# Converting the last weight group three units later, with its partial words in PSUM, and starting the second network's weights one half chunk later

## The chip, the cores and the metric

The kernel runs on one core of one Trainium2 chip. The metric is the device time of one execution in microseconds (us). Three runs of the kernel before took 775.98, 778.04 and 781.6 us; the median is 778.04. The profiled execution took 776.87 us, and its span, from the first to the last instruction, is 775.0 us.

## The reference: what is computed

A linear attention with decay runs over four batches, eight heads and 768 steps; its output is a matrix of 3072 tokens by 384. Two feed-forward networks follow, one after the other.

```python
state = alpha[:, :, t, :, None] * state + np.einsum('bhd,bhe->bhde', k[:, :, t], v[:, :, t])
y[:, :, t] = np.einsum('bhd,bhde->bhe', q[:, :, t], state)
...
h = x @ w_in                                   # 384 -> 2048
P = a[0] + a[1] * h + a[2] * h2 + a[3] * h3    # h2 = h*h, h3 = h2*h
Q = 1.0 + np.abs(b[0]) * np.abs(h) + np.abs(b[1]) * h2
x = (P / (Q + 1e-06)) @ w_out                  # 2048 -> 384
...
h = x @ w_in                                   # 384 -> 1024
solu = h * softmax(h)
(layernorm(solu) * g_ln) @ w_out               # 1024 -> 384
```

The weights of both networks arrive as 64-bit floats. The kernel makes 32-bit words of them with integer operations, and then two rounded parts, a high and a low one, for TensorE.

## The kernel before

**Chunks, units, halves.** The steps are cut into six chunks of 128 steps, 512 tokens each. The first network's 2048 columns are cut into 16 pieces of 128. One piece of one chunk is a *unit*: u0 to u95, u0 to u15 being chunk 0. `m_up` runs a unit's nine matmuls into a tile `hp` (line 592; three PSUM banks rotate), then the rational function on ScalarE and VectorE (lines 597 to 625) and the low part on GpSimd (line 626). `m_down` (line 638) runs nine matmuls for a unit four units earlier. The last VectorE operation of a unit is line 616 (even units below 24) or line 623 (all others).

**The attention** runs beside the units, two *halves* to a chunk. Half h2 is started at u2, h3 at u10, h4 at u18 and so on; halves h2 and h3 make the input `xt` of chunk 1, that is of u16 to u31. `a_pe` makes, for a half, four score tiles `sc` (line 420), which ScalarE copies (line 427) and GpSimd masks (line 428), two tiles `y` (line 444), from which ScalarE and VectorE write `xt` (lines 470, 471), and the update tile `u` (line 483, read by line 493). All of `sc`, `y` and `u` are tiles of one PSUM pool with the tag `at`, which has **two** banks. `a_dve` (lines 300 to 338) prepares the half after that on VectorE: transposes (290, 295, 324), scans (308, 317) and products (320).

**Weight conversion.** The first network's weights are four groups, g0 to g3; group n serves units 4n to 4n+3 of every chunk. `w1_group` makes a group in seven *splits*: three of 512 columns from `w_in`, needed by the units' up matmuls, and four of 384 columns from `w_out`, needed by the down matmuls. A split (`split_w`) is a load into a staging tile `st` (line 533; two buffers), three VectorE operations with the partial word between them (537, 540, 541), a copy on ScalarE (547) and a subtraction on GpSimd (548). Where the partial word lies is said by `stage["bank"]`:

```python
if stage["bank"] == "x2":
    fp = ps_x2p.tile(...)          # PSUM, tag x2p
elif stage["bank"] == "at":
    fp = ps_ap.tile([128, NTOK], F32, name="fp", tag="at")
else:
    fp = ft                        # SBUF, in place
```

Groups g0 and g1 are made before u0, g2 at units 0 to 3 in the banks `at`, g3 at units 4 to 7 in place in SBUF. The second network's weights are 14 splits more (`w2_split`), which go back to DRAM; the main loop takes one at each unit u >= `U2` whose number is 0 or 7 modulo 8, with the partials in the banks `at`.

**Order.** Each engine and each DMA queue works through a fixed list. A scheduler that has its own idea of durations sets these lists when the kernel is built; it keeps what the program's order and `issue_after` demand and otherwise sorts freely. So a change in one place of the loop moves instructions on all engines. Loads are issued by SyncE (SP) in order: one that waits for its buffer holds up all behind it.

Of the kernel before, what the change touches and what calls it, by code (L numbers as in the profile page):

```python
# [23 lines left out]
def _run(*gens):  # L24
    for g in gens:
        for _ in g:
            pass
# [3 lines left out]
def kernel(  # L31
# [25 lines left out]
    NF1 = DF1 // 128  # L57
# [19 lines left out]
    G1 = 99  # L77
# [3 lines left out]
    SKIP = (5, 7, 11)  # L81
    AHEAD = 3
    LATE = 2
    U2, IDLE = NF1 - 1, (0, NF1 // 2 - 1)
    assert (B, H, D, CH) == (4, 8, 48, 128)

    const = ctx.enter_context(tc.tile_pool(name="const", bufs=1, side="left"))
# [55 lines left out]
    def judge(moe_pool):  # L143

        sums = const.tile([128, 1], F32, name="sums")
        row = moe_pool.tile([1, 128], F32, name="row", tag="ft", bufs=2)
        tot = const.tile([1, 1], F32, name="tot")
        nc.vector.tensor_reduce(sums, bad, axis=AX.X, op=ALU.add)
        nc.sync.dma_start(out=row, in_=sums)
        nc.vector.tensor_reduce(tot, row, axis=AX.X, op=ALU.add)  # L150
        nc.vector.tensor_scalar(flag, tot, 0.0, None, ALU.is_gt)

    def network(fast):
# [351 lines left out]
        stage = {"n": 0, "wide": False, "near": False, "bank": None}  # L505
# [46 lines left out]
        def w1_group(n):  # L552
            w = moe_pool.tile([128, GW], F32R, name=f"g{n}", tag=f"g{n}")
            hi, lo = (w[:, 512 * KT * x:512 * KT * (x + 1)].rearrange("p (a b) -> p a b", a=KT) for x in range(2))
            for kt in range(KT):
                split_w(moe_w_in[128 * kt:128 * kt + 128, 512 * n:512 * n + 512], hi[:, kt, :], lo[:, kt, :])
                yield
            wi[n] = (hi, lo)
            hi, lo = (w[:, 4 * DM * x:4 * DM * (x + 1)].rearrange("p (a b) -> p a b", a=4) for x in range(2, 4))
            for f in range(4):  # L560
                r0 = 512 * n + 128 * f
                split_w(moe_w_out[r0:r0 + 128, :], hi[:, f, :], lo[:, f, :])
                yield
            wo[n] = (hi, lo)
# [9 lines left out]
        def x_load(c):  # L574
            for kt in range(KT):
                nc.sync.dma_start(
                    out=x_tile(c)[:, kt].rearrange("p a t -> p (a t)").bitcast(F32), in_=y_d[c][128 * kt:128 * kt + 128, :]
                )
# [50 lines left out]
        def m_down(u):  # L629
            c, f = divmod(u, NF1)  # L630
            n, o = divmod(f, 4)
            if f == 0:
                x2ps[c] = [ps_x2p.tile([128, NTOK], F32, name=f"x2p{d}", tag=f"x2p{d}") for d in range(KT)]
            gh, gl = gts.pop(u)
            hi, lo = wo[n]
            for d in range(KT):
                for w, gg in ((hi, gh), (hi, gl), (lo, gh)):
                    nc.tensor.matmul(  # L638
                        x2ps[c][d], lhsT=w[:, o, 128 * d:128 * d + 128], rhs=gg,
                        start=(f == 0 and w is hi and gg is gh), stop=(f == NF1 - 1 and w is lo),  # L640
                    )
            if f == NF1 - 1:
                for d0, n in ((0, 2), (2, 1)):
                    e = moe_pool.tile([128, 2, NTOK], F32, name="x2e", tag="st", bufs=2)
                    for d in range(n):
                        nc.scalar.activation(e[:, d], x2ps[c][d0 + d], AF.Copy, scale=back if fast else 1.0)  # L646
                    nc.sync.dma_start(out=x2_d[c][:, d0:d0 + n, :], in_=e[:, :n])
                del x2ps[c]
# [14 lines left out]
        def w2_load(nm):  # L663
            src = {"i": w2i_d, "o": w2o_d}[nm]
            n, step = {"i": (KT, 1), "o": (NF2, 4)}[nm]
            for z in range(0, n, step):
                for x, y in enumerate("hl"):
                    nc.sync.dma_start(out=w2[nm + y][:, z:z + step].bitcast(F32), in_=src[:, x, z:z + step])
                    yield
# [3 lines left out]
        def n_load(c):  # L673
            t = x2s[c] = moe_pool.tile([128, KT, 2, NTOK], F32R, name="x2", tag="xt", bufs=2)
            for kt in range(KT):
                raw = t[:, kt, 1].bitcast(F32)
                nc.sync.dma_start(out=raw, in_=x2_d[c][:, kt, :])
                nc.scalar.activation(t[:, kt, 0], raw, AF.Copy)
                nc.gpsimd.tensor_tensor(t[:, kt, 1], raw, t[:, kt, 0].bitcast(F32), ALU.subtract)
                yield  # L680

        def open2():
            if fast:
                ps_a.__exit__(None, None, None)
            ph2["ps_pool"] = tc.tile_pool(name="ps_e", bufs=1, space=PSUM, side="right", reuse_waits="tile")
            ph2["ps"] = ph2["ps_pool"].__enter__()
            if fast:
                att.__exit__(None, None, None)
            ph2["pool"] = tc.tile_pool(name="w2", bufs=1, side="right", reuse_waits="tile")
            pool = ph2["pool"].__enter__()  # L690
            for nm, dims in (("i", [128, KT, DF2]), ("o", [128, NF2, DM])):
                for y in "hl":
                    w2[nm + y] = pool.tile(dims, F32R, name="w2" + nm + y)
# [102 lines left out]
        def take(g, n):  # L796
            for _ in range(n):
                if next(g, "end") == "end":
                    return False
            return True  # L800

        def chain(*gens):
            for g in gens:
                yield from g
# [37 lines left out]
        def later(n):  # L842
            return tc.issue_after(fin[now[0] - n].ins) if n <= now[0] < GE + n and now[0] - n in fin else ExitStack()
# [9 lines left out]
        def half_steps(i):  # L853
            gp = a_pe(i)
            gd = chain(a_prep(i + 1), a_move_qk(i + 1) if i + 1 >= NPE else iter(()), a_load(i + 2, ("ra", "rk")) if i + 2 < NH and i + 1 >= NPE else iter(())) if i + 1 < NH else iter(())
            while True:
                with pin(GP):
                    a = next(gp, "end")
                with pin(GS):
                    b = next(gd, "end")  # L860
                    if b != "end":
                        b = next(gd, "end")
                if a == "end" and b == "end":
                    if i + 1 < NH:
                        _run(a_enter(i + 1))
                        if i + 2 < NH and i + 1 < NPE:
                            _run(a_load(i + 2))
                    return
                yield
# [4 lines left out]
        prep = iter(())  # L874
        for u in range(NU + LAG):
            c, f = divmod(u, NF1)
            now[0] = u
            if f % (NF1 // 2) == LATE and u < NU:
                _run(side)
                i = 2 * c + 2 + f // (NF1 // 2)  # L880
                side = half_steps(i) if fast and i < NH else iter(())
            if u < NU:
                if f == 0 and c == NCH - 1:
                    if fast:
                        judge(moe_pool)
                    open2()
                    tail = chain(w2_load("i"), n_load(0), w2_load("o"))
                if f == 0 and c and not fast:
                    x_load(c)
                if fast and u < NF1:  # L890
                    if f % 4 == 0:
                        _run(prep)
                        if f:
                            stage["near"] = False
                            stage["bank"] = ""
                        prep = w1_group(f // 4 + 2) if f < 8 else iter(())
                    with later(G1):
                        take(prep, 1)
                m_up(u)
                if fast and u < NF1:  # L900
                    with later(G1):
                        take(prep, 1)
            if u == NU:
                _run(n_load(1))
            take(side, 1)
            if u >= U2 and f % (NF1 // 2) in IDLE:
                stage["bank"] = "at"
                with later(G2):
                    take(split2, 1)
            if tail is not None:  # L910
                _run(split2)
                take(tail, 2)
            if u >= LAG:
                m_down(u - LAG)
            if u - NU + NF1 in EARLY:
                n_tile(EARLY.index(u - NU + NF1))
                if len(EARLY) == B and u - NU + NF1 == EARLY[-1]:
                    n_turn(0)
# [141 lines left out]
```

## Time and profile before

| | |
|---|---|
| median of three runs | 778.04 us |
| profiled execution | 776.87 us, its span 775.0 us |
| busy: TensorE / VectorE / ScalarE / GpSimd | 728.0 / 630.4 / 535.2 / 358.4 us |
| last VectorE operation of u0, u8, u16, u24 ends at | 79.2, 123.8, 168.6, 210.7 us |
| the same for u72, u80, u88 | 460.7, 499.2, 537.3 us |

Times in a trace are counted from the span's start. An engine's row in the page's slices gives its busy share in tenths. A matmul's end is modelled and matmuls overlap, so that a TensorE that is busy all the time need not be at its peak; how many matmuls run in a stretch says more. `PE` is TensorE, `DVE` VectorE, `ACT` ScalarE, `POOL` GpSimd, `SP` SyncE.

### The profile page before, as it was taken

How to read it: one execution, taken by the hardware profiler on the slowest of the kernel's cores; microseconds unless marked ns; L12 is line 12 of the kernel's file. 1: busy time of each engine (PE TensorE's matmuls, PEld its weight loads, DVE VectorE, ACT ScalarE, POOL GpSimd, SP SyncE). 2: the span in 40 equal slices, each digit the busy share in tenths (PEclk: the TensorE clock that was granted, in tenths of full speed). 3: DMA queues.
4: the chain of work that ended last, by engine and by line, in shares of the span. 5: the costliest groups of instructions: out<-in, count | busy, mean ns of one | idle time of the engine just before them, and what ended most of it. 6: DMA issues, size and time to landing. Idle time of an engine off the chain costs nothing.

```text
span 775.0 us, 13914 instructions
## 1 busy us (share of the span) xinstructions
PE 728.0 (94%) x4976; PEld 605.8 (78%) x4976; DVE 630.4 (81%) x1110; ACT 535.2 (69%) x983; POOL 358.4 (46%) x306
## 2 busy tenths in 40 slices
PE   4676999999999999999999999999999999999996
PEld 3565767788888787778877788888888989988986
DVE  4999999989898989899898966478887788877640
ACT  2245867689878888788878887788965545555541
POOL 3255777777554355434444433332243343452322
PEclk9857899999999999999999999999999999999999
DMA  7995446466837382727554350720025253542653
GB/s 167 253 275 165 107 155 167 146 147 206 204 99 161 122 205 83 172 66 207 137 148 91 124 82 1 296 112 0 1 83 132 89 130 90 132 108 52 140 119 76
DMA packets 87278, 101.74 MB, mean 131 GB/s; under 512 B 34464, under 2 KB 63136, under 8 KB 87200
## 3 DMA queue, kind: packets, MB, share of 16 engines
q1 hardware_dynamic: 87104, 100.67, 48.9%
q8 instruction: 41, 0.67, 0.4%
q14 instruction: 37, 0.30, 0.1%
q10 hardware_dynamic: 96, 0.10, 0.0%
HBM read 60.59 MB, written 27.56 MB: 114 GB/s over the span
## 4 chain that ended last, share of the span: by engine, by line
DVE 30%; PE 18%; ACT 12%; issue 5%; SPq 3%; DMA 3%; POOL 1%; ACTq 0%; DVEq 0%; POOLq 0%
PE x2p L638 6%; PE hp L592 6%; DVE room L752 3%; SPq L762 3%; DVE room L735 2%; DVE p L618 2%; ACT jk L737 2%; PE op L776 2%; DVE hp L622 2%; DVE w L621 2%; DMA room<-room 2%; DVE sm L731 2%; DVE room L750 2%; PE h L712 2%; DVE p L623 2%
## 5 line engine op out<-in xcount | busy, mean ns | idle before, releaser
L592 PE MATMUL hp<-xt,g 128*128 128x512 f32 x864 | 224.1, 401 | 14.8 <-DVE p L616 7.5
L626 POOL TENSOR_TENSOR gl<-p,gh 128x512 fp32r<-128x512 f32 x96 | 130.8, 1362 | 193.9 <-ACT gh L625 107.9
L592 PEld LDWEIGHTS hp<-xt,g 128*128 128x128 f32 x864 | 163.2, 192 | 54.2 <-DVE p L616 7.7
L638 PE MATMUL x2p<-gh,g 128*128 128x512 f32 x576 | 196.9, 395 | 2.0 <-ACT x2e L646 2.0
L638 PEld LDWEIGHTS x2p<-gh,g 128*128 128x128 f32 x576 | 107.9, 188 | 29.1 <-ACT x2e L646 4.7
L638 PE MATMUL x2p<-gl,g 128*128 128x512 f32 x288 | 112.9, 392 | 0.0
L776 PE MATMUL op<-w2oh,room 128*128 128x384 f32 x384 | 101.8, 339 | 1.3 <-ACT room L767 0.7
L768 POOL TENSOR_TENSOR room<-room,room 128x1024 fp32r<-128x1024 f32 x22 | 54.8, 2496 | 101.0 <-ACT room L767 79.0
L621 DVE SCALAR_TENSOR_TENSOR w<-w,co,hp 128x512 f32<-128x512 f32 x84 | 62.0, 738 | 43.5 <-ACT hp L620 42.5
L712 PE MATMUL h<-w2ih,x 128*128 128x512 f32 x288 | 90.7, 394 | 0.0
L599 ACT ACTIVATE p<-hp,co 128x512 f32<-128x512 f32 x96 | 66.0, 687 | 12.3 <-POOL gl L626 12.0
L620 ACT ACTIVATE hp<-ah 128x512 f32<-128x512 f32 x84 | 50.1, 597 | 33.3 <-DVE p L618 32.0
L776 PEld LDWEIGHTS op<-w2oh,room 128*128 128x128 f32 x384 | 70.1, 188 | 3.0 <-ACT room L767 1.0
L600 ACT ACTIVATE w<-ah,co 128x512 f32<-128x512 f32 x96 | 69.4, 724 | 1.7 <-DVE hp L622 1.3
L618 DVE SCALAR_TENSOR_TENSOR p<-p,co,hp 128x512 f32<-128x512 f32 x84 | 61.6, 734 | 9.3 <-ACT p L599 9.0
L597 ACT ACTIVATE ah<-hp 128x512 f32<-128x512 f32 x96 | 56.7, 591 | 16.4 <-PE hp L592 16.0
L776 PE MATMUL op<-w2ol,room 128*128 128x384 f32 x192 | 65.0, 339 | 0.0
L625 ACT ACTIVATE gh<-p 128x512 fp32r<-128x512 f32 x96 | 59.9, 623 | 5.7 <-DVE p L623 2.8
L638 PEld LDWEIGHTS x2p<-gl,g 128*128 128x128 f32 x288 | 54.1, 188 | 11.7 <-issue 0.8
L712 PEld LDWEIGHTS h<-w2ih,x 128*128 128x128 f32 x288 | 53.9, 188 | 11.7
L623 DVE SCALAR_TENSOR_TENSOR p<-p,co,hp 128x512 f32<-128x512 f32 x84 | 61.9, 737 | 1.1
L619 ACT ACTIVATE ah<-w,co 128x512 f32<-128x512 f32 x84 | 60.6, 721 | 1.3
(168 smaller groups left out, 1264.7 us busy)
## 6 DMA issues: line engine op xcount, KB each, us to landing
room<-room SPq DMA_DIRECT2D x96, 128.0 KB, 2.3
qk_d<-qk SPq DMA_DIRECT2D x10, 771.0 KB, 4.1
st<-in_moe_w_in_dram SPq DMA_DIRECT2D x13, 512.0 KB, 4.6
st<-in_moe_w_out_dram SPq DMA_DIRECT2D x16, 384.0 KB, 3.5
qks<-qk_d SPq DMA_DIRECT2D x20, 257.0 KB, 4.4
x<-x_d SPq DMA_DIRECT2D x18, 256.0 KB, 3.1
out_dram<-o SPq DMA_DIRECT2D x94, 48.0 KB, 1.6
ra<-in_alpha_dram SPq DMA_DIRECT2D x44, 96.0 KB, 2.8
```

What stands on the lines that cost most here:

```text
L592: last["PE", u] = nc.tensor.matmul(hp, lhsT=w[:, kt, 128 * o:128 * o + 128], rhs=xts[c][:, kt, xx, :], start=(kt == 0 and w is hi and xx = ...
L599: nc.scalar.activation(p, hp, AF.Square, bias=co[:, 7:8])
L600: nc.scalar.activation(w, ah, AF.Square, bias=co[:, 6:7])
L618: nc.vector.scalar_tensor_tensor(p, p, a1, hp, ALU.add, ALU.mult)
L619: nc.scalar.activation(ah, w, AF.Ln, bias=rest)
L621: nc.vector.scalar_tensor_tensor(w, w, rest, hp, ALU.add, ALU.mult)
L623: fin[u] = nc.vector.scalar_tensor_tensor(p, p, a0, hp, ALU.add, ALU.mult)
L625: last["ACT", u] = nc.scalar.activation(gh, p, AF.Copy)
L626: last["POOL", u] = nc.gpsimd.tensor_tensor(gl, p, gh[:].bitcast(F32), ALU.subtract)
L638: nc.tensor.matmul(x2ps[c][d], lhsT=w[:, o, 128 * d:128 * d + 128], rhs=gg, start=(f == 0 and w is hi and gg is gh), stop=(f == NF1 - 1 an ...
L712: nc.tensor.matmul(hp[:, 512 * n:512 * n + 512], lhsT=x2s[c][:, kt, x, CH * b:CH * b + CH], rhs=w2[w][:, kt, 512 * n:512 * n + 512], start ...
L776: nc.tensor.matmul(op, lhsT=x[:, 128 * f:128 * f + 128], rhs=w2[w][:, f, :], start=(f == 0 and x is hi and w == "oh"), stop=(f == NF2 - 1 ...
```

## The change

Group g3 is begun at u7 instead of u4, so that its seven splits are taken two to a unit at u7 to u10, and its partial words stay in the banks `at` as those of g2 do. `U2` becomes 23 instead of 15, so that the 14 splits of the second network's weights are taken at u23, u24, u31, u32 and so on to u71, u72, where before they were taken at u15, u16 to u63, u64. The calls that ask `issue_after` are left out; with `G1` = 99 they had no effect.

```diff
-    U2, IDLE = NF1 - 1, (0, NF1 // 2 - 1)
+    OPEN3 = 7
+    U2, IDLE = NF1 + NF1 // 2 - 1, (0, NF1 // 2 - 1)
...
-                if fast and u < NF1:
-                    if f % 4 == 0:
-                        _run(prep)
-                        if f:
-                            stage["near"] = False
-                            stage["bank"] = ""
-                        prep = w1_group(f // 4 + 2) if f < 8 else iter(())
-                    with later(G1):
-                        take(prep, 1)
+                if fast and u == 0:
+                    prep = w1_group(2)
+                if fast and u == OPEN3:
+                    _run(prep)
+                    stage["near"] = False
+                    prep = w1_group(3)
+                take(prep, 1)
                 m_up(u)
-                if fast and u < NF1:
-                    with later(G1):
-                        take(prep, 1)
+                take(prep, 1)
```

Lines of the changed file are numbered one higher than before up to the main loop: 420 is 421 there, 537 is 538.

**TensorE around the scores of half h3, before.** The first score tile, `sc_1388`, stands ahead of u11's up matmuls (`hp_1427`), right after the update of half h2.

```order
L483 MATMUL u_1209<-vns_115,kns_113 64x48 x16
L420 MATMUL sc_1388<-qks_112 128x128 x4
L638 MATMUL x2p2_1096<-gh_1197,g1_629 128x512
L638 MATMUL x2p2_1096<-gl_1198,g1_629 128x512
L638 MATMUL x2p2_1096<-gh_1197,g1_629 128x512
L592 MATMUL hp_1427<-xt_356,g2_751 128x512 x9
```

The same tiles in the change are `sc_1395`, `sc_1396`, `sc_1460`, `sc_1461`; `hp_1713` is u15, `gh_1456` is u11 and `gh_1519` is u12.

```order
L639 MATMUL x2p2_1079<-gl_1457,g2_751 128x512
L639 MATMUL x2p2_1079<-gh_1456,g2_751 128x512
L421 MATMUL sc_1395<-qks_112 128x128 x4
L421 MATMUL sc_1396<-qks_112 128x128 x4
L421 MATMUL sc_1460<-qks_112 128x128 x4
L593 MATMUL hp_1713<-xt_356,g3_1195 128x512 x9
L421 MATMUL sc_1461<-qks_112 128x128 x4
L639 MATMUL x2p0_1077<-gh_1519,g3_1195 128x512
```

All four score tiles have moved behind the ups of u11 to u14 and the downs of u8 to u11; they stand directly ahead of u15.

**VectorE after the last operation of u11, in the change.** `fp_1289`, `fp_1307`, `fp_1342` and `fp_1360` are the partial words of g3's four splits of 384 columns; The lines 296 to 325 prepare half h4; in the rows left out stand the rest of the split of `fp_1289`, the split of `fp_1307`, one small transpose and one operation each of u12 and u13.

```order
L538 TENSOR_SCALAR fp_1289<-st_1290 128x384
L321 TENSOR_TENSOR qk_1476<-qk_1476,alT_111 128x2x3x128
L541 SCALAR_TENSOR_TENSOR fp_1289<-st_1290,fp_1289 128x384
L325 STREAM_TRANSPOSE alT_111<-qk_1476 128x3x4x32 x2
L296 STREAM_TRANSPOSE qk_1476<-rq_1418 128x4x32 x2
...
L538 TENSOR_SCALAR fp_1342<-st_1343 128x384
L541 SCALAR_TENSOR_TENSOR fp_1342<-st_1343,fp_1342 128x384
L542 SCALAR_TENSOR_TENSOR ft_1341<-st_1343,fp_1342 128x384
L538 TENSOR_SCALAR fp_1360<-st_1361 128x384
L541 SCALAR_TENSOR_TENSOR fp_1360<-st_1361,fp_1360 128x384
L542 SCALAR_TENSOR_TENSOR ft_1359<-st_1361,fp_1360 128x384
```

In the kernel before, all 21 conversion operations of g3 stood ahead of u11's last operation; now 12 of them stand behind it. `fp_1342` and `fp_1360` are the tiles that hold the two banks `at` just before `sc_1395` and `sc_1396`.

**VectorE at the border of chunk 0 and chunk 1.** Before, `xt_1078` is written ahead of two splits of the second network's weights (`fp_1738`, `fp_1784`) and of most of u14 (`hp_1644`) and u15 (`p_1718`).

```order
L471 TENSOR_TENSOR xt_1078<-y_1519,xt_1078 128x256
L537 TENSOR_SCALAR fp_1738<-st_1736 128x512
L540 SCALAR_TENSOR_TENSOR fp_1738<-st_1736,fp_1738 128x512
L610 SCALAR_TENSOR_TENSOR hp_1644<-p_1656,co_85,hp_1644 128x512
L541 SCALAR_TENSOR_TENSOR ft_1737<-st_1736,fp_1738 128x512
L537 TENSOR_SCALAR fp_1784<-st_1782 128x512
```

In the change `p_1725` is u15, `hp_1751` u16 and `p_1799` u17.

```order
L624 SCALAR_TENSOR_TENSOR p_1725<-p_1725,co_85,hp_1713 128x512
L472 TENSOR_TENSOR xt_1061<-y_1525,xt_1061 128x2x256
L472 TENSOR_TENSOR xt_1061<-y_1526,xt_1061 128x256
L494 TENSOR_TENSOR Sbd_114<-Sbd_114,u_1678 48x8x48 x2
L611 SCALAR_TENSOR_TENSOR hp_1751<-p_1763,co_85,hp_1751 128x512
L619 SCALAR_TENSOR_TENSOR p_1799<-p_1799,co_85,hp_1787 128x512
```

The two splits are gone from here, and `xt` is now written after the last operation of u15, with one pair of updates between it and u16's first.

## Rows read from the trace of the kernel before

**Rows 1.** The page's slices: busy tenths in 40 slices of 19.4 us.
```profile
PE   4676999999999999999999999999999999999996
DVE  4999999989898989899898966478887788877640
```

**Rows 2.** Windows: length, busy us and instructions of each engine, clock, DMA share, GB/s.
```profile
101.65:148.51 46.86, 42.47 (x343) 32.79 (x342) 46.34 (x75) 33.56 (x62) 36.98 (x33) 0.96 0.59 165
148.51:168.63 20.12, 20.06 (x176) 16.42 (x177) 17.49 (x30) 15.60 (x28) 15.71 (x14) 1.00 0.82 205
168.63:210.71 42.08, 42.08 (x334) 34.17 (x334) 37.48 (x62) 36.93 (x68) 27.62 (x25) 1.00 0.68 183
210.71:419.49 208.78, 204.37 (x1613) 163.33 (x1612) 190.67 (x311) 171.43 (x312) 98.16 (x90) 1.00 0.54 140
460.71:499.19 38.48, 38.48 (x315) 31.62 (x314) 23.89 (x34) 30.52 (x53) 12.69 (x13) 1.00 0.28 100
499.19:745.00 245.81, 245.81 (x1172) 214.52 (x1171) 187.76 (x348) 156.63 (x295) 92.14 (x54) 1.00 0.35 94
```

**Rows 3.** Window of tile ft alone: DVE, ACT and POOL of g3's conversion.
```profile
101.58:143.10 41.52, 17.65 (x22) 3.98 (x7) 8.79 (x7) 0.96 0.62 172
```

**Rows 4.** Groups by line and shape, partials in PSUM: busy us, mean ns, idle before.
```profile
L540 DVE SCALAR_TENSOR_TENSOR fp<-st,fp 128x512 int32<-128x512 int32 x10 | 6.9, 690 | 0.2
L537 DVE TENSOR_SCALAR fp<-st 128x512 int32<-128x512 int32 x10 | 6.9, 688 | 1.2 <-DMA st<-in_moe_w_in_dram 0.6 <-ACT lent L396 0.5
L541 DVE SCALAR_TENSOR_TENSOR ft<-st,fp 128x512 int32<-128x512 int32 x10 | 6.8, 680 | 0.1
L540 DVE SCALAR_TENSOR_TENSOR fp<-st,fp 128x384 int32<-128x384 int32 x12 | 6.8, 564 | 0.2
L537 DVE TENSOR_SCALAR fp<-st 128x384 int32<-128x384 int32 x12 | 6.7, 557 | 0.2
L541 DVE SCALAR_TENSOR_TENSOR ft<-st,fp 128x384 int32<-128x384 int32 x12 | 6.6, 547 | 0.2
```

**Rows 5.** DVE timeline, g3's first two TENSOR_SCALARs: start, us, engine, line, shapes.
```profile
101.58 0.41 DVE L537 TENSOR_SCALAR ft<-st 128x512 int32<-128x512 int32 x1
...
107.38 1.58 DVE L537 TENSOR_SCALAR ft<-st 128x512 int32<-128x512 int32 x1
```

**Rows 6.** DVE timeline, preparation of half h4 and u11's last operation.
```profile
143.65 0.95 DVE L320 TENSOR_TENSOR qk<-qk,alT 128x768 f32<-128x768 f32 x1
144.52 0.74 DVE L610 SCALAR_TENSOR_TENSOR hp<-p,co,hp 128x512 f32<-128x512 f32 x1
145.18 0.68 DVE L622 SCALAR_TENSOR_TENSOR hp<-w,hp 128x512 f32<-128x512 f32 x1
145.78 1.63 DVE L324 STREAM_TRANSPOSE alT<-qk 128x384 f32<-128x384 f32 x2
147.32 0.67 DVE L295 STREAM_TRANSPOSE qk<-rq 128x128 f32<-128x128 f32 x2
147.84 0.67 DVE L623 SCALAR_TENSOR_TENSOR p<-p,co,hp 128x512 f32<-128x512 f32 x1
```

**Rows 7.** DVE timeline: xt of half h3, then u16's first operation.
```profile
153.17 1.01 DVE L471 TENSOR_TENSOR xt<-y,xt 128x512 fp32r<-128x512 f32 x2
...
166.07 0.76 DVE L610 SCALAR_TENSOR_TENSOR hp<-p,co,hp 128x512 f32<-128x512 f32 x1 [1.66 <-ACT p L599]
```

**Rows 8.** Timelines of PE and ACT: h3's first and last scores, last copy, u16's ups.
```profile
125.38 1.16 PE L420 MATMUL sc<-qks 48*128 48x128 f32 x8
...
140.06 1.16 PE L420 MATMUL sc<-qks 48*128 48x128 f32 x8
...
144.67 0.58 ACT L427 ACTIVATE A<-sc 128x512 f32<-128x512 f32 x1
...
160.00 2.20 PE L592 MATMUL hp<-xt,g 128*128 128x512 f32 x9
```

**Rows 9.** The chain of waits, one unit's nine matmuls at full clock: start, us.
```profile
450.37 2.04 PE hp L592 x9
```

**Rows 10.** DMA issues of 85 to 165 us: KB each, median us to landing.
```profile
st<-in_moe_w_out_dram SPq DMA_DIRECT2D x4, 384.0 KB, 3.1
```

**Rows 11.** Windows of 2 us around a pause of TensorE, columns as in rows 2.
```profile
108.00:110.00 2.00, 0.33 (x1) 0.30 (x2) 2.00 (x3) 0.35 (x1) 1.46 (x2) 1.00 0.79 226
110.00:112.00 2.00, 2.00 (x6) 1.61 (x5) 2.00 (x4) 1.91 (x4) 1.63 (x2) 0.51 1.06 366
```

## The prediction

> **What bounds the kernel now.** I read the slices first, then the windows cut at the last VectorE operations of u11, u16, u24, u64, u72 and u80. In the slices VectorE is at nine tenths until the eighth slice, and TensorE from the sixth on [rows 1]. The windows say it by stage [rows 2]. From 101.65 us to u11's end VectorE is busy for 46.34 of 46.86 us and TensorE for 42.47; in the next stretch, to u16's end, VectorE is at 17.49 of 20.12 and TensorE at 20.06. From then on TensorE is full: 42.08 of 42.08, 204.37 of 208.78, 38.48 of 38.48, 245.81 of 245.81. So two rules follow. What shortens VectorE's list before u16 can bring u16 forward, as long as no wait on TensorE takes its place. And what u16 gains or loses is carried to the end, since no stage behind it has idle time on TensorE to make it good; only work that TensorE did earlier can be given back.
>
> **Term 1, cheaper partial words.** The window of the tile `ft` has the cost of g3's conversion: 17.65 us of VectorE in 22 operations, one of them the tail of another group, so about 17.6 for 21 [rows 3]. With the partial word in PSUM the same three operations take 0.688, 0.690 and 0.680 us at 512 columns and 0.557, 0.564 and 0.547 at 384 [rows 4]. Three splits at 2.058 are 6.17 us, four at 1.668 are 6.67, together 12.84: **-4.8 us** of VectorE. ScalarE's and GpSimd's share (3.98 and 8.79 us [rows 3]) is moved, not changed.
>
> The saving depends on where time is lost in SBUF. The two first operations of g3 have the same shape and took 0.41 and 1.58 us [rows 5]: short, or long beside something else. The Trainium skill, "VectorE: DVE Perf Modes", section "Why PSUM operands drop a tier", says that an operand in PSUM holds a 32-bit operation at the basic rate; here the 0.41 us in SBUF against 0.688 in PSUM agrees. That speaks against the change, and what it would make of the sum stands under the rivals. The sum goes by 17.6 us, since that is the mean of the stretch in which these operations run.
>
> **Term 2, the second network's first two splits** leave the border of the chunks: two splits of 512 columns, 2 x 2.06 = **4.1 us** of VectorE before u16's end. Every other pair moves by eight units too. They come back at u71 and u72, where VectorE has 38.48 - 23.89 = 14.6 us of idle time [rows 2]; that hides them, with their loads and stores. If the cover is gone (VectorE late in another stretch), two splits of 384 columns cost 3.3 us there. I take +0.5.
>
> **Term 3, the stretch up to u11.** Three of g3's splits (6.17 us) stay ahead of u11's last operation, four go behind it. Removed are 17.6 - 6.2 = 11.4 us; part of the preparation of h4 goes behind too, 0.95 + 1.63 + 0.67 = 3.25, and one of u12's operations, 0.74 [rows 6]. VectorE's 46.34 becomes 46.3 - 11.4 - 3.25 - 0.74 = 30.9 us; with the old idle time of 0.5, u11 would end at 133.1. TensorE can't quite follow: each unit asks two times nine matmuls, 2 x 2.04 = 4.08 us [rows 9], and the attention beside them, and it was busy for 42.47 us of this stretch [rows 2]. What moves off it are three of the four score tiles and their followers. I add 2 to 6 us of idle time on VectorE: u11 ends at 135 to 139, taken as 137, 11.5 earlier than before.
>
> **Term 4, the new wait.** Before, the first score tile of h3 was made at 125.38 us and the last at 140.06 [rows 8]; `xt`, which all of chunk 1 needs, was written at 153.17 to 154.18 [rows 7]. Now the tiles `fp_1342` and `fp_1360` of g3's sixth and seventh splits hold the two banks `at`. The score tiles come behind them, and these splits stand behind u11's last operation. Ahead of the first score tile VectorE works through 15 rows: three splits (3 x 1.668 = 5.0), four rows of preparation (0.95, 1.63, 0.67, and 0.67 for the fourth by its neighbour) and two operations of units (2 x 0.74), 10.4 us by their durations and 9.4 by their starts, since [rows 6] show starts a tenth closer than the durations. To this comes about 1 us, since a staged load needs 3.1 us to land [rows 10] and there are two buffers. The first score tile can start at 137 + 9.4 + 1 = **147.4**, the second three operations later at 149. The third waits for a bank too, some 1.2 us after that; the fourth has u15's nine matmuls ahead of it (2.04 us) and ends near 153.5.
>
> From the last score tile to the end of `xt` it took 154.18 - 140.06 - 1.16 = 13.0 us before, of which the last copy waited for ScalarE until 144.67 [rows 8]; from that copy on it is 9.5. So `xt` is done between 163 and 166.5, I take 164.5: 10 us later than before.
>
> u16's up matmuls need `xt`. They started at 160.00 before, 5.8 us after it was there; now they stand behind u15's last operations with nothing else to wait for. Its last operation came 8.6 us after the start of its ups (168.63 - 160.00). With up to 2.7 us for twelve down matmuls ahead of it, u16 ends at 164.5 + 8.6 + (0 to 2.7) = 173 to 176, and by the ends of `xt` at 171.6 to 177.8. I take **175**, 6.4 us later. Terms 1 and 2 are inside that: they let u11 come 11.5 us earlier, and the wait swallows it. VectorE's own work from u11 to u16 is 17.49 - 4.1 + 6.67 + 3.25 + 0.74 + 1.47 (two operations of u17 now ahead) = 25.5 us; from 137 that is 162.5, so 12 us of idle time lie in this stretch.
>
> **Sum.** At u16 +6.4; TensorE has by then done up to 18 down matmuls that it did later before, which gives back 1 of their 4.1 us, since the first units of a chunk are held by VectorE and ScalarE as well; at u71 +0.5. That is +5.9, taken as +6: the profiled 776.87 becomes 782.9. The median shown is 1.2 us above the profiled execution, so **784.0**. What a measurement of this kernel can tell from no change is about 1%, 7.8 us.
>
> **The rivals.**
> - *The savings hold (faster).* If the two banks come free early, because VectorE reaches g3's sixth split by 138 or 139, `xt` is ready by 154 and u16 ends at 162.5 to 164 by VectorE's work alone: -5 to -6, 772 to 774. For it: VectorE's list is 4.8 + 4.1 us shorter. Against: the order itself puts the last 12 of 21 conversions behind u11, and TensorE has no room to bring u11 to 128. The point where it turns: `xt` before 155. Chance 0.10.
> - *It evens out.* The wait is there, but matmuls done earlier and a stage from u16 to u24 without the second pair of splits win back 5 to 7 us: 776 to 780. For it: VectorE is at 37.48 of 42.08 there, 4.1 of it a pair. Against: that pair is only replaced by the one eight units earlier at u23 and u24, and TensorE is full. Chance 0.20.
> - *The wait costs more (slower).* Each of the two last loads waits in full, 2 x 3.1 us instead of 1, or TensorE's pause ahead of the first score tile, 4 us by this sum, costs it its clock: after a pause of about 2 us the granted clock was 0.51 in the next 2 us window, the lower of its two levels, 1.2 GHz [rows 11]. Each such stretch of 4 us loses 2. u16 then ends 10 to 12 us later: 788 to 791. Chance 0.22.
> - *PSUM partials cost more, not less (slower).* If g3's operations, at other units, would have run in SBUF as the short one did (0.41 us, and about 0.31 at 384 columns), PSUM adds 9 x 0.28 + 12 x 0.25 = 5.5 us to the 7.3 they would take. This would show only beside a kernel with both, since here 17.6 us are on the trace; taken as -4.8 turned into +1.8, u16 comes 6.6 us later still: 790. The skill's rule alone would say so; the 17.65 us speak against it. Chance 0.03.
>
> My forecast, 778 to 788, has 0.45. The chances of the cases sum to 1. The range reaches from 777, which takes in the upper two thirds of evening out, to 790: left out are the savings (0.10), the lowest part of evening out (0.05) and the top of the slower two (0.05). Faster by over 1% would be below 770.3; the best rival stops at 772 and only its tail reaches that: 0.05. Slower by over 1% is above 785.8: the slower rivals (0.22 + 0.03) and a sixth of the main case, 0.32. Within 1%: 0.63.
>
> **What the changed kernel's profile would show.** g3's 21 operations at 12.8 us in all (term 1). u11's last operation at 135 to 139 (term 3). The first score tile of h3 near 147, released by VectorE's third operation of g3's sixth split, with TensorE idle ahead of it (term 4). `xt` at 163 to 166.5, u16's last operation at 172 to 178. From there a constant distance to the times before, about 6 us, at u24, u64 and u80, and the stage u72 to u80 no longer than 38.5 us (term 2).
>
> Wrong it would be if the score tiles start before 140, if the distance at u16 shrinks stage by stage, or if VectorE rather than TensorE ends the stages behind u16.

## The result and the profile after

The change is slower: 789.42 us (787.45 to 791.5, four runs) against 777.16 us, a ratio of 1.0146 with a 95% interval of 1.0115 to 1.0177, which is 9 to 14 us. The profiled execution, 791.5 us with a span of 789.7, is the longest of the four.

The windows of the changed kernel, from 94.80 and then cut at the last VectorE operations of u11, u16, u24, u64, u72, u80 and near the end, answer to [rows 2] (same columns). The row from u64 to u72 is left out.

```profile
94.80:137.70 42.90, 40.44 (x304) 31.86 (x302) 38.52 (x65) 28.95 (x53) 28.61 (x25) 1.00 0.47 127
137.70:179.24 41.54, 34.75 (x282) 28.29 (x283) 25.85 (x44) 26.30 (x48) 23.95 (x23) 0.88 0.40 105
179.24:220.40 41.16, 39.24 (x314) 31.39 (x312) 37.53 (x60) 33.60 (x61) 26.80 (x24) 1.00 0.65 180
220.40:428.30 207.90, 203.33 (x1596) 162.63 (x1596) 191.28 (x311) 170.28 (x311) 98.72 (x89) 1.00 0.56 144
...
471.30:508.80 37.50, 37.50 (x308) 30.76 (x305) 23.91 (x35) 30.14 (x53) 12.86 (x13) 1.00 0.29 104
508.80:754.60 245.80, 245.74 (x1170) 214.10 (x1169) 187.77 (x345) 156.35 (x295) 91.58 (x54) 1.00 0.34 93
```

The second row has the loss. From u11's end to u16's it takes 41.54 us where it took 20.12, TensorE is busy for 34.75 of them only, and its granted clock there is 0.88. u11 ends at 137.70 (10.8 us earlier than before), u16 at 179.24 (10.6 later). After that the distance hardly changes: 9.7 at u24, 8.8 at u64, 10.6 at u72, 9.6 at u80 and at u95. In the profiled execution another 5.0 us are added behind u95. A part of these distances lies ahead of the change: the end of u0 lies between 76.8 and 79.2 us over the profiled executions of all fourteen kernels, at 79.2 in the kernel before and at 77.6 in the change.

TensorE's timeline has the pause (start, us, line, shapes; in brackets the idle time ahead). It answers to [rows 8].

```profile
148.55 2.04 PE L421 MATMUL sc<-qks 48*128 48x128 f32 x8 [5.05 <-issue]
152.27 3.07 PE L421 MATMUL sc<-qks 48*128 48x128 f32 x16 [1.68 <-issue]
155.27 3.94 PE L593 MATMUL hp<-xt,g 128*128 128x512 f32 x9
159.13 1.16 PE L421 MATMUL sc<-qks 48*128 48x128 f32 x8
167.90 0.84 PE L593 MATMUL hp<-xt,g 128*128 128x512 f32 x3
```

The first score tile of half h3 starts at 148.55 after 5.05 us of idle time, the second and third at 152.27, and u15's nine matmuls (155.27) take 3.94 us where nine take 2.04 [rows 9]. u16's ups start at 167.90.

VectorE's timeline says what they waited for: the last two splits of g3, `xt`, and u16's last operation.

```profile
146.63 0.56 DVE L538 TENSOR_SCALAR fp<-st 128x384 int32<-128x384 int32 x1 [0.36 <-DMA st<-in_moe_w_out_dram]
...
147.89 0.55 DVE L542 SCALAR_TENSOR_TENSOR ft<-st,fp 128x384 int32<-128x384 int32 x1
150.35 0.56 DVE L538 TENSOR_SCALAR fp<-st 128x384 int32<-128x384 int32 x1 [1.90 <-DMA st<-in_moe_w_out_dram]
...
151.61 0.55 DVE L542 SCALAR_TENSOR_TENSOR ft<-st,fp 128x384 int32<-128x384 int32 x1
...
165.80 1.02 DVE L472 TENSOR_TENSOR xt<-y,xt 128x512 fp32r<-128x512 f32 x2 [0.69 <-ACT xt L471]
...
178.56 0.68 DVE L617 SCALAR_TENSOR_TENSOR p<-w,hp 128x512 f32<-128x512 f32 x1
```

The third operation of the sixth split ends at 148.44, 0.11 us ahead of the first score tile; that of the seventh at 152.16, 0.11 ahead of the second. Both splits waited for their staged loads, as SP's queue shows (start, us from the first issue to the last).

```profile
132.46 4.96 SPq L534 DMA_DIRECT2D st<-in_moe_w_out_dram  x2
...
143.33 0.33 SPq L534 DMA_DIRECT2D st<-in_moe_w_out_dram  x1
143.87 1.28 SPq L267 DMA_DIRECT2D ra<-in_alpha_dram  x3
145.26 0.37 SPq L534 DMA_DIRECT2D st<-in_moe_w_out_dram  x1
```

The sixth split's load goes out at 143.33, when the fourth split has given its staging buffer back (its third operation ends at 143.30). The seventh's goes out at 145.26, when the fifth's has (144.97) and three loads of `ra` have gone ahead; its data are used at 150.35, 5.1 us later. All of that is the load: it took 5.1 us from issue to landing, with the loads of `ra` and the store of `qk` under way beside it. The fifth split's load, issued at 137.07 with nothing beside it, took 3.0.

The clock around the pause, in windows of 2 us (columns as in [rows 2]):

```profile
146.00:148.00 2.00, 0.00 (x0) 0.00 (x0) 1.50 (x4) 1.23 (x3) 2.00 (x3) 1.00 0.74 112
148.00:150.00 2.00, 1.45 (x7) 1.48 (x8) 0.45 (x1) 1.52 (x3) 1.16 (x2) 0.63 0.94 351
150.00:152.00 2.00, 0.59 (x3) 0.29 (x2) 1.51 (x3) 0.01 (x1) 1.31 (x2) 0.50 0.75 273
...
156.00:158.00 2.00, 2.00 (x7) 1.52 (x6) 0.13 (x1) 2.00 (x5) 1.85 (x2) 0.50 0.00 0
158.00:160.00 2.00, 2.00 (x11) 1.52 (x10) 0.76 (x1) 0.90 (x3) 2.00 (x4) 0.81 0.00 0
```

After the pause TensorE has half its clock (0.50, the lower level of 1.2 GHz) until about 159 us.

Last, term 1 by itself: g3's 21 operations, as the window of the tile `st` gives them (DVE, ACT, POOL).

```profile
117.70:152.20 34.50, 12.77 (x21) 0.00 (x0) 0.00 (x0) 0.95 0.56 155
```

12.77 us, where it was 17.65 with one more operation [rows 3].

### The profile page after: what moved, and what is told of

Its sections match the earlier page's. It is cut to its first block, busy times and chain, and to the rows that moved or that the text cites. A ratio compares the mean times of both kernels' runs of the same rounds, so it can differ in the third digit from the quotient of the medians.

```text
span 789.7 us, 13915 instructions
## 1 busy us (share of the span) xinstructions
PE 734.6 (93%) x4976; PEld 610.8 (77%) x4976; DVE 630.6 (80%) x1110; ACT 534.1 (68%) x983; POOL 353.9 (45%) x306
## 4 chain that ended last, share of the span: by engine, by line
DVE 40%; PE 24%; ACT 14%; issue 8%; DMA 7%; SPq 5%; POOL 2%; ACTq 0%; DVEq 0%; POOLq 0%
PE hp L593 9%; PE x2p L639 8%; DVE room L753 3%; SPq L763 3%; DVE w L622 3%; PE op L777 2%; DVE p L624 2%; DVE hp L623 2%; DVE room L736 2%; DVE p L619 2%; ACT jk L738 2%; PE sc L421 2%; DMA room<-room 2%; DVE room L751 2%; DVE sm L732 2%
## 5 line engine op out<-in xcount | busy, mean ns | idle before, releaser
L777 PE MATMUL op<-w2oh,room 128*128 128x384 f32 x384 | 104.2, 345 | 3.3 <-ACT room L768 2.6
L777 PEld LDWEIGHTS op<-w2oh,room 128*128 128x128 f32 x384 | 71.9, 193 | 5.2 <-ACT room L768 3.0
L598 ACT ACTIVATE ah<-hp 128x512 f32<-128x512 f32 x96 | 56.7, 591 | 26.0 <-PE hp L593 21.3
```

The source lines that it names most:

```text
L777: nc.tensor.matmul(op, lhsT=x[:, 128 * f:128 * f + 128], rhs=w2[w][:, f, :], start=(f == 0 and x is hi and w == "oh"), stop=(f == NF2 - 1 ...
```

## The experiments

All runs are compared with runs of the kernel before on the same chip (its median there is 777.2 us for the change and 777.6 to 778.1 for e1 to e12). "Last split" is the end of g3's 21st conversion operation, "first score" the start of h3's first score tile, "xt" and "u16" the end of the last VectorE operation of each, "clock" the granted clock from 148 to 156 us; all of these come from each kernel's profiled execution.

| run | g3 from | partial words | pairs from | median us | ratio [95%] | first score | last split | xt | u16 | clock |
|---|---|---|---|---|---|---|---|---|---|---|
| before | u4 | SBUF | u15 | 777.2 | 1 | 125.4 | 143.1 | 154.2 | 168.6 | 1.00 |
| the change | u7 | banks `at` | u23 | 789.4 | 1.015 [1.012, 1.018] | 148.5 | 152.2 | 166.8 | 179.2 | 0.53 |
| e1 | u4 | SBUF | u23 | 781.2 | 1.004 [1.001, 1.006] | 122.3 | 140.5 | 151.6 | 166.3 | 1.00 |
| e2 | u7 | banks `at` | u15 | 790.5 | 1.017 [1.013, 1.020] | 146.7 | 151.2 | 166.1 | 179.0 | 0.50 |
| e3 | u7 | SBUF | u23 | 782.5 | 1.006 [1.003, 1.008] | 123.3 | 143.0 | 153.5 | 167.9 | 1.00 |
| e4 | u7 | banks of `hp` | u23 | 779.1 | 1.002 [0.999, 1.004] | 135.2 | 136.4 | 155.3 | 171.7 | 1.00 |
| e5 | u4 | banks `at` | u15 | 774.1 | 0.997 [0.994, 0.999] | 141.8 | 145.7 | 157.0 | 170.3 | 1.00 |
| e6 | u7, filled | banks `at` | u23 | 792.3 | 1.018 [1.015, 1.022] | 148.5 | 152.0 | 172.2 | 186.0 | 0.65 |
| e7 | u7 | banks of `hp` | u15 | 776.1 | 0.998 [0.996, 1.000] | 132.7 | 133.9 | 152.9 | 169.7 | 1.00 |
| e8 | u4 | banks of `hp` | u15 | 785.8 | 1.011 [1.006, 1.015] | 140.0 | 129.5 | 162.2 | 180.3 | 1.00 |
| e9 | u7 | five `at`, two SBUF | u23 | 789.9 | 1.014 [1.010, 1.018] | 142.1 | 152.4 | 164.5 | 177.4 | 0.50 |
| e10 | u5 | banks `at` | u15 | 792.2 | 1.017 [1.014, 1.020] | 148.7 | 157.5 | 171.7 | 184.6 | 0.50 |
| e11 | u4 | five `at`, two SBUF | u15 | 781.1 | 1.004 [1.002, 1.007] | 136.8 | 147.6 | 158.0 | 171.8 | 1.00 |
| e12 | u4 | banks `at` | u23 | 781.7 | 1.004 [1.002, 1.006] | 143.9 | 146.3 | 158.9 | 171.4 | 1.00 |

### e1 to e4: which part, and which bank

e1, against the kernel before:

```diff
-    U2, IDLE = NF1 - 1, (0, NF1 // 2 - 1)
+    U2, IDLE = NF1 + NF1 // 2 - 1, (0, NF1 // 2 - 1)
```

> The kernel before with the second network's splits begun at u23 instead of u15 and nothing else. Theory (the two banks of the scores' pool cost the time): this edit alone takes 4.1 us of VectorE away ahead of u16, the order of h3's score tiles stays that of before, so u16 ends 3 to 4 us earlier and the run takes 773 to 775 us. Rival 1 (the late second network's weights are what costs): 780 us or more. Rival 2 (TensorE is full behind u16 and the pair was covered): 777 us, no change.

Measured: 0.4% slower. By its time that is rival 1. At u16 it is rival 2: the distance to before is -2.3 us there and already -1.9 at u0, so the pair was covered. The theory's 4.1 us are nowhere.

e2, against the change:

```diff
-    U2, IDLE = NF1 + NF1 // 2 - 1, (0, NF1 // 2 - 1)
+    U2, IDLE = NF1 - 1, (0, NF1 // 2 - 1)
```

> The change without its second part: g3 at units 7 to 10 with partial words in the scores' banks, the second network's splits still from u15. Theory: all of the loss comes from here, u16 ends 8 to 12 us later than before (the two splits now stand behind xt and are not covered any more) and the run takes 788 to 793 us. Rival 1 (the other part is the cause): 772 to 777 us.

As the theory said: g3's part alone gives the whole loss, with the same first score, `xt` and u16 within 2 us.

e3, against the change:

```diff
                     stage["near"] = False
+                    stage["bank"] = ""
```

> The change, but g3's partial words lie in SBUF in place as before; its unit (u7) and the start at u23 stay as in the change. Theory (banks): the first score tile of h3 stands ahead of u11 again and starts near 125 us, u16 ends 3 to 4 us earlier than before, 773 to 775 us. Rival 3 (weights converted three units later make u12 to u15 late, whatever the bank): u16 ends as in the change, near 177 us, 787 to 790 us.

Begun at u7 but in SBUF, g3 costs next to nothing beyond e1: the score tiles and g3's last split come when they came before, since the scheduler puts them in the old places. So e3 does not test rival 3: in SBUF the later unit did not make the conversion later. u16 comes only 0.7 us earlier (1.0 at u0), and the run is 8 us longer than the theory said, as e1 was.

e4, against the change:

```diff
+            elif stage["bank"] == "h":
+                fp = ps_hp.tile([128, NTOK], F32, name="fp", tag="h")
...
                     stage["near"] = False
+                    stage["bank"] = "h"
```

> The change, but g3's partial words lie in the three rotating PSUM banks of the up matmuls instead of the two of the scores; all else as in the change. Theory (it is the scores' banks, and the cheaper word of term 1 is real): h3's score tiles start before 135 us, g3's 21 operations take 13 us, u16 ends 3 to 8 us earlier than before, 769 to 775 us. Rival 3 (late conversion): 787 to 790 us. Rival 4 (a shared bank costs wherever it is: the ups of u7 to u11 wait for VectorE's third operations): u11 or u12 comes 3 us or more later, u16 near that of before or later, 777 to 782 us.

Between the theory and rival 4: the first score tile is early (135.2), g3 is done at 136.4, but the ups wait (u7 ends 9.2 us later, TensorE idles 7.5 us from 118.1) and u16 is 3.1 later; 779.07 us. So far "the banks of the scores" stood.

### e5 to e8: bank without the later unit, and TensorE's pause

e5, against the change (e2's line too):

```diff
-    OPEN3 = 7
+    OPEN3 = 4
```

> The kernel before with g3's partial words in the scores' two banks and nothing else: still begun at u4, the second network's splits still from u15. Theory (the bank decides, not the unit): h3's score tiles come behind g3's last splits as in the change, after 143 us, u16 ends 6 to 11 us later than before, 784 to 790 us. Rival (the three units later decide, and a PSUM word alone is term 1's gain): u16 ends 3 to 5 us earlier, 772 to 776 us.

**The theory falls.** The banks alone make the kernel *faster*, 774.14 us, though the score tiles do come late, at 141.8, and u16 1.7 us later. Not the bank and not the unit, but both together cost the time. With the pairs from u23 the table has all four kernels: 781.2 (neither, e1), 782.5 (the unit, e3), 781.7 (the bank, e12) and 789.4 (both, the change). Together is also where the last split ends late: at 151.2 or later in the five slow kernels (the change, e2, e6, e9, e10), at 147.6 or earlier in the nine others. TensorE's timeline of e5, from the update of half h2 to u15's ups:

```profile
137.78 1.14 PE L484 MATMUL u<-vns,kns 128*64 128x48 f32 x32 [3.28 <-issue]
...
141.83 1.16 PE L421 MATMUL sc<-qks 48*128 48x128 f32 x8
...
146.35 1.71 PE L421 MATMUL sc<-qks 48*128 48x128 f32 x16
147.99 2.34 PE L593 MATMUL hp<-xt,g 128*128 128x512 f32 x9
```

VectorE's timeline of e5, the last operation of g3 and `xt`:

```profile
145.13 0.55 DVE L542 SCALAR_TENSOR_TENSOR ft<-st,fp 128x384 int32<-128x384 int32 x1
...
156.00 1.02 DVE L472 TENSOR_TENSOR xt<-y,xt 128x512 fp32r<-128x512 f32 x2
```

SP's queue in e5, g3's last load:

```profile
137.70 0.35 SPq L534 DMA_DIRECT2D st<-in_moe_w_out_dram  x1
```

Windows of e5 from u11 to u16 and from u24 to u64 (columns as in [rows 2]):

```profile
138.30:170.30 32.00, 31.32 (x295) 24.82 (x292) 22.32 (x39) 23.11 (x41) 24.95 (x25) 1.00 0.74 186
209.00:416.80 207.80, 205.81 (x1619) 166.15 (x1619) 189.72 (x312) 172.19 (x316) 99.01 (x90) 1.00 0.56 143
```

The last load goes out 7.6 us earlier than in the change, g3 is done 6.5 us earlier, and TensorE is busy for 31.32 of 32.00 us from u11 to u16 at full clock (in the change 34.75 of 41.54 at 0.88). From u16 (+1.7) to u80 (-4.0) it wins 5.6 us. By u16's end it has begun 136 of the down matmuls, where before it was 120; but the change had begun 138 and won only 1.0 us by u80. So work done ahead is not the whole of it, and where the rest comes from is not settled.

e6, against the change:

```diff
-            for kt in range(KT):
+            for kt in [k for _ in range(3 if u == 14 else 1) for k in range(KT)]:
```

> The change with u14's nine matmuls run three times over into the same tile (the last pass gives the result), which fills 4.1 us of TensorE's pause ahead of h3's first score tile and changes nothing else of what is computed. Theory (part of the loss is the clock that TensorE lost by that pause): the idle time falls from 5.05 us to about 1 us, the granted clock stays 1.00 from 148 to 159 us, a score tile takes 1.16 us and u15's nine matmuls 2.04 again, u16 ends 3 to 4 us earlier than in the change (near 175.5 us), the run takes 784 to 787 us. Rival (only the order of waits counts, or the clock falls in any case): u16 as in the change, 788 to 792 us.

Neither. The pause ahead of the first score tile shrinks from 5.05 to 0.88 us and the clock is 1.00 until 150, but then the second score tile waits 2.46 us for the seventh split, and the clock falls all the same (TensorE's timeline, then windows with the columns of [rows 2]):

```profile
148.52 1.13 PE L421 MATMUL sc<-qks 48*128 48x128 f32 x8 [0.88 <-issue]
152.10 3.07 PE L421 MATMUL sc<-qks 48*128 48x128 f32 x16 [2.46 <-issue]
```

```profile
148.00:150.00 2.00, 1.13 (x8) 0.96 (x8) 0.41 (x1) 1.55 (x4) 1.35 (x2) 1.00 0.96 360
150.00:152.00 2.00, 0.00 (x0) 0.00 (x0) 1.68 (x4) 0.49 (x1) 1.87 (x3) 0.62 0.72 266
...
162.00:164.00 2.00, 2.00 (x20) 1.45 (x13) 0.07 (x1) 1.88 (x3) 1.88 (x2) 0.50 0.03 8
```

`xt` comes at 172.2, since the order around it moved too. How much of the loss is the clock alone stays open.

e7 (e4 with e2's line) and e8 (e7 with e5's line):

> As the run with g3's partial words in the three banks of the up matmuls (779.07 us, begun at u7), but with the second network's splits from u15 as before. Theory (the later start of those splits costs some 3 us by itself, as the run with that edit alone said): 775 to 777 us. Rival (it costs nothing, and the 781.19 us of that run were other stages): 779 us or more, since 4.1 us of VectorE come back ahead of u16.

776.1 us, as the theory said: the pairs from u15 are 3 us better than from u23.

> Only g3's partial words moved into the three banks of the up matmuls, begun at u4 and with the second network's splits from u15, both as before. If VectorE's 4.8 us (term 1) are worth their time once no score tile waits: u16 ends 4 to 5 us earlier, 772 to 774 us. If the stages from u8 to u16 are bound by the attention's chain and by TensorE rather than by VectorE's sum: no change, 776 to 779 us. If the shared banks hold up the up matmuls: 780 us or more.

785.82 us: the shared banks hold up the ups (u7 ends 21.3 us late).

### e9 to e12: the wait itself

e9, against the change:

```diff
             for f in range(4):
+                if n == 3 and f == 2:
+                    stage["bank"] = ""
                 r0 = 512 * n + 128 * f
```

> The change, but the last two of g3's seven splits (those whose partial words hold the two banks just before h3's score tiles) keep their partial words in SBUF; the other five stay in the banks. Theory (the score tiles wait for these two splits, each of which waits for its staged load): the first score tile starts near 143.5 us, with the third operation of the fourth split, the second near 145, u16 ends 2 to 5 us later than before instead of 10.6, the run takes 778 to 783 us. Rival (the late conversion itself holds u12 to u16, through the down matmuls that need g3): u16 as in the change, 787 to 790 us.

The rival is right by its time, 789.9 us; its way, through the down matmuls, is not what the timeline shows. The score tiles are freed, the first starts 6.5 us earlier, and it helps `xt` by 2.4 us and u16 by 1.9. ScalarE's timeline shows what holds them now (the copies of the last two scores, and of the high parts of the last two splits):

```profile
148.32 0.52 ACT L548 ACTIVATE g<-ft 128x384 fp32r<-128x384 f32 x1 [0.97 <-DVE ft L542]
148.75 0.58 ACT L428 ACTIVATE A<-sc 128x512 f32<-128x512 f32 x1
...
152.43 0.52 ACT L548 ACTIVATE g<-ft 128x384 fp32r<-128x384 f32 x1 [2.62 <-DVE ft L542]
152.86 0.58 ACT L428 ACTIVATE A<-sc 128x512 f32<-128x512 f32 x1
```

ScalarE's list has the seventh split's copy ahead of the last score's copy, and VectorE's list has that split ahead of the ends of u12 and u13. Both wait in order for one late split. Meanwhile TensorE idles and runs at 0.50. But the edit did two things: that split, now in SBUF, takes 3.34 us from its first operation to the end of its third (1.81 in the change), as VectorE's timeline of e9 shows:

```profile
149.06 1.17 DVE L538 TENSOR_SCALAR ft<-st 128x384 int32<-128x384 int32 x1 [0.78 <-DMA st<-in_moe_w_out_dram]
...
151.53 0.87 DVE L542 SCALAR_TENSOR_TENSOR ft<-st,ft 128x384 int32<-128x384 int32 x1
```

It starts 1.3 us earlier than in the change and ends 0.2 later. What the freed banks would give with the cheaper words no run shows.

e10 is e2 with `OPEN3 = 5`.

> g3 begun at u5, one unit later than before, with partial words in the scores' banks and the second network's splits from u15. With u4 this took 774.14 us and the first score tile came at 141.8 us, with u7 790.51 us and 146.7 us. Theory (bank and unit act together: each unit later moves the last two splits and with them the score tiles): the first score tile at 143 to 145 us, 776 to 782 us. Rival (a threshold: the order is that of u4 or that of u7): 774 or 789 us.

The expected range is missed: 792.18 us, worse than with u7, so the rival's step is nearer. One unit is enough to bring the seventh split's load to 148.54: the fifth split gives its staging buffer back at 148.17, and three loads of `ra` go out ahead, as SP's queue in e10 shows:

```profile
147.16 1.29 SPq L267 DMA_DIRECT2D ra<-in_alpha_dram  x3
148.54 0.38 SPq L534 DMA_DIRECT2D st<-in_moe_w_out_dram  x1
```

In VectorE's timeline of e10 the third operations of the fifth and sixth splits stand first, as one row; the seventh split waits 3.58 us for its load and ends at 157.52:

```profile
147.63 1.00 DVE L542 SCALAR_TENSOR_TENSOR ft<-st,fp 128x384 int32<-128x384 int32 x2
...
152.87 0.56 DVE L538 TENSOR_SCALAR fp<-st 128x384 int32<-128x384 int32 x1 [3.58 <-DMA st<-in_moe_w_out_dram]
...
156.97 0.55 DVE L542 SCALAR_TENSOR_TENSOR ft<-st,fp 128x384 int32<-128x384 int32 x1
```

e11 is e5 with e9's two lines, meant as a better version.

> g3 begun at u4 as before, five splits with partial words in the scores' banks, the last two in SBUF, second network's splits from u15: meant as the better version. If the score tiles still wait for the last two splits in the run with u4 and all seven in the banks (774.14 us): they start near 138 us, xt is ready by 154, and the run takes 770 to 773 us. If TensorE is full at that border anyway (it was, from 144 us on): 773 to 776 us, no gain over it.

It is not: 781.1 us. The score tiles start 5.0 us earlier than in e5, but the last split ends 1.9 later and `xt` 1.0 later. Here too that split is dearer in SBUF: its three operations take 3.6 us where e5 has 1.7.

e12 is e5 with the pairs from u23.

> g3 at u4 with partial words in the scores' banks (774.14 us), and the second network's splits from u23 as in the change. If VectorE still held u16 there, 4.1 us less would show at u16: 770 to 772 us. If the pair is covered at the border (TensorE is full) and is paid later instead, where it moves into other stages: 774 to 778 us.

781.72 us, 7.6 above e5. The late pairs bring nothing at u16 here either and are paid for later, more than I had expected.

## Why the prediction was right, and where its sizes were off

The direction, the place and the range held; the forecast of +6 came out as +9 to +14. The range held narrowly: 789.42 lies 0.6 us inside its upper end, and two of the four runs lie above it. In part that is chance, since the profiled execution has 5.0 us of its loss in a place that the sum did not have (last point below).

- **Term 1** held: 12.84 us forecast, 12.77 measured. The rival that partial words in PSUM cost more is out: in e9 the last two splits, at the change's later units but in SBUF, took 6.0 us of VectorE, in the change 3.3. (That rival also gave all 21 operations the short time. Only three came shorter in SBUF than in PSUM, all of them first operations of a split; the fastest of the others took 0.68 us at 512 columns and 0.54 at 384.) e5, with that edit alone, is 0.35% faster; that this is the saving itself is not shown, since u16 ends 1.7 us later in it. Why SBUF is dearer: the 1.58 us operation of [rows 5] ran while GpSimd worked on one of its own, and ended 0.28 us after it (GpSimd's timeline before):

```profile
106.95 1.73 POOL L335 TENSOR_TENSOR qk<-qk,P 128x768 f32<-128x768 f32 x1 [1.22 <-DVE qk L290]
```

  The Trainium skill, "SBUF — State Buffer", section "SBUF: two separate sides", says that VectorE in its two-port mode and GpSimd share a pair of ports that one of them holds for a whole instruction. The seven first operations of g3 agree: the three that took 0.33 to 0.41 us started ahead of GpSimd's operation or 0.11 us before one ended, and the four that took 0.78 to 1.58 ended 0.2 to 0.3 us after a two-input one. They make up only 1.6 of the 4.9 us saved. The rest comes from the second and third operations, which read two tiles: nine of these fourteen took longer in SBUF than the fastest of their size, and each of the nine ended 0.41 to 0.55 us after an operation of GpSimd.

- **Term 3** held: u11 at 137.70, forecast 137. But 1.6 us had been won by u0's end already (77.6 against 79.2), which is no part of the term.

- **Term 4** is the one mis-sized. Of the 4.2 us that u16 came later than forecast (179.24 against 175), 1.1 were there at the first score tile (148.55 against 147.4), 1.2 came up to `xt` (166.8 against 164.5) and 1.9 between `xt` and u16, where the ups of u16 stop after three of nine for the update tile of h3 (1.14 us at 168.67). `xt` and u16 both came just past the ranges given for them. I had allowed 1 us for the staged loads. VectorE waited 0.36 and 1.90 us for them, since the last load took 5.1 us to land where 3.1 had been taken, the second score tile came at 152.27 instead of 149, and the clock, which I had put into a rival only, doubled the time of u15's matmuls. That rival's time, 788 to 791, is where the run came out.

- **The reason given in term 4 was too narrow.** I wrote that the banks hold the score tiles. They do, to 0.11 us. But e9 freed them with little gain (1.9 us at u16, none in the median), and e5 held them without loss. What e9 shows is a late last split ahead of much else in VectorE's and ScalarE's lists; the held banks are one of several queues behind it. In ten of the eleven kernels with no word in the banks of `hp`, `xt` ends 10.4 to 14.9 us after g3's last split, at whatever time the first score tile comes (122 to 149); where the column "clock" has 1.00 it is 10.4 to 12.6. The eleventh, e6, has 20.2. That this split sets `xt` in all of them is inferred from these ends; in e9 the copy of the last score is seen to wait behind it. No run makes the last split late without any word in the banks `at`, so what the lateness alone costs stays open.

- **Term 2** failed as a gain: the pair was covered at the border (e1, e12). Its price later was right in place and about right in size in the profiles: in all seven kernels with pairs from u23 the distance to before grows by 0.7 to 1.3 us from u64 to u80 (I took 0.5), in the six with pairs from u15 by nothing, or shrinks. But e1, e4 against e7, and e12 against e5 lose 3, 3 and 7.6 us by the medians, while the change against e2 loses nothing (-1.1). Of the 9.2 us between the spans of the profiled executions of e12 and e5, 5.4 are there at u95, 2.0 come in the second network's chain and 1.8 at the very end; e2, with the pairs from u15, has these last two as well, so they do not go with the pairs. Where the rest goes is not settled; the profiled execution of e1 is its shortest of twelve.

- **"What u16 loses is carried to the end"** held for the change (10.6 at u16, 9.6 at u95) and not as a rule: e5 was 1.7 us late at u16 and 4.0 early at u80. The rows had 4.4 us of idle time on TensorE between u24 and u64 [rows 2], which the rule passed over; in e5 it is 2.0. (TensorE's slices [rows 1] are at nine tenths from the fifth on, not the sixth; nothing hangs on it.)

- **Not in the sum at all** were 5.0 us behind u95 in the profiled execution: 2.2 in the second network's chain on VectorE, and 2.8 at the very end, where TensorE ran out of work and lost its clock again. Windows of 5 us there (clock 0.79 and 0.52):

```profile
760.00:765.00 5.00, 1.92 (x6) 1.60 (x7) 1.23 (x1) 2.47 (x3) 0.00 (x0) 0.79 0.92 207
765.00:770.00 5.00, 5.00 (x18) 5.00 (x17) 0.00 (x0) 1.08 (x2) 4.46 (x2) 0.52 0.73 169
```

## What to carry to other kernels

When a step that feeds a border of the pipeline is moved later, find the last instruction of that step and list what stands behind it on *every* engine in order, its loads included; freeing the one resource that the trace names was not enough in e9. The cheaper operations paid only where the step neither ended late nor took banks from the ups (e8): the same PSUM words in the scores' banks gained 0.35% when begun at u4 and cost 1.7% when begun one unit later (e10). So e5 is the version to keep, 774.14 us, faster than both kernels.

## What the runs showed of the hardware

- A VectorE operation on 128x1 elements can take 2.3 us. In the second network three operations of one chain met GpSimd's subtractions in the change. Two of them in VectorE's timeline:

```profile
643.01 2.34 DVE L749 SCALAR_TENSOR_TENSOR sm<-sm 128x1 f32<-128x1 f32 x1
...
645.58 2.89 DVE L751 TENSOR_SCALAR room<-room,sm 128x1024 f32<-128x1024 f32 x1
```

GpSimd's timeline beside the last one:

```profile
645.52 2.40 POOL L769 TENSOR_TENSOR room<-room,room 128x1024 fp32r<-128x1024 f32 x1 [0.19 <-ACT room L768]
```

  Before, the last of the three just missed GpSimd's next one (it started 0.14 us ahead of it) and took 0.81 us. VectorE's timeline before:

```profile
635.81 0.81 DVE L750 TENSOR_SCALAR room<-room,sm 128x1024 f32<-128x1024 f32 x1
```

GpSimd's timeline before:

```profile
635.95 2.93 POOL L768 TENSOR_TENSOR room<-room,room 128x1024 fp32r<-128x1024 f32 x1 [0.19 <-ACT room L767]
```

  This is the step of 2.2 us; e2, e9 and e12 have it too, and e4, with the same order of VectorE there as the change, has not. By these starts it is a matter of 0.2 us of timing.

- Half the clock goes with the loss: the five kernels with 0.50 to 0.65 from 148 to 156 us took 789 to 792 us by the median, the nine with 1.00 there 774 to 786. That does not make the clock the cause: the last split ends late in the same five, and e4, at 779.1 us, had 0.50 from 124 to 130 us. A pause of 3.3 us ahead of the update tile and u14's ups in e5 cost no clock, one of 2.5 us in e6, with eight short matmuls between it and the pause before, did.
